# A three-layer kernel on one core: first token block undivided, six pairs of w_in prepared in it, and a maximum in the weight conversion

## Chip, cores and metric

The kernel runs on one core of a Trainium2 chip. The metric is the device time of one execution in microseconds; the time before is the median of three runs.

## What is computed

The reference runs a linear attention over 8 batches of 8 heads (576 tokens, head dimension 64), and then two dense layers over the 4608 tokens, with a SiLU and with a hard swish. Inputs are fp32; the weights reach the chip as 64-bit numbers.

```python
q_s = np.exp(q - q.max(-1, keepdims=True)); q_s = q_s / (q_s.sum(-1, keepdims=True) + 1e-09)
k_s = np.exp(k - k.max(2, keepdims=True));  k_s = k_s / (k_s.sum(2, keepdims=True) + 1e-09)
kv = np.einsum('bhsd,bhse->bhde', k_s, v)
x = np.einsum('bhsd,bhde->bhse', q_s, kv)          # then laid out as 4608 x 512
h = x @ w_in;  x = (h / (1 + np.exp(-h))) @ w_out            # 512 -> 2048 -> 512
h = x @ w2_in; out = (h * np.clip(h + 3, 0, 6) / 6) @ w2_out
```

## The kernel before

Tokens go in nine blocks of 512: eight hold the first 512 tokens of a batch, the ninth the remaining 64 of each. A layer has 8 pairs p of hidden slices (2 x 128). A *cycle* g is one pair of one block of one layer: 144 cycles, of which the first 8 (`first_cycle`) are block 0 of layer 1 and the other 136 (`cycle`) all the rest. A cycle computes the first product of its pair (x times w_in) into the PSUM banks A, B and C, the activation of both halves (`bend`), and, one cycle late, the second product (`layer_out`, called G(0) to G(7)) of the pair before, into four accumulating banks y.

Exactness is kept by splitting an fp32 operand into a rounded high part and the remainder (`split`: a cast on ScalarE, then a subtraction on VectorE), and doing three matmuls for one (`mm3`, lines 73 to 75). In `cycle` the first product is done as seven half-size products in place of eight (`product` 1 to 7), which needs sums of x (`sums_x`), their splits (`operand_x`), and sums of w_in (`operands_w`: four additions or subtractions of 256 columns, a split of 768 columns and one of 1024), kept in one of two `ring` tiles. `prepare_in(p)` makes such a ring tile and `keep_w` writes it to DRAM (`wd`); later blocks read it back with `load_w(g)`, two cycles ahead.

Block 0 is different. Its second product is one full fp32 matmul (line 550, which the trace shows as two instructions), on weights that are not split. Its first product (`plain_in`) is undivided in the sense of the seven products, but each factor is split: x by `at_xhalf` into op tiles, w_in by `plain_w` into a ring tile. Pairs 0 and 1 are made ready for the later blocks in cycles 6 and 7, pairs 2 to 7 in the cycles 8 to 13 of block 1, two cycles before their use; block 1 uses all eight from the ring tile where they were made, without reading them back.

Weights arrive as 64-bit bit patterns (`feed`, 1 MB each), and `converting` makes fp32 of them: an absolute value of the high word on ScalarE (line 103), then on VectorE a shift (104), the sign (109), the low word's bits (114), and a multiplication by a comparison, which sets tiny weights to zero (121). These steps lie between `yield`s; `pump(k)` advances the oldest unfinished generator by k steps at fixed places in a cycle.

Attention for later blocks runs in between. Unit u is one pair of heads of one batch (32 units). `plan` gives each of its steps a tick relative to x_at(u), eight ticks a cycle, and `run(tick)` issues them at the place `side(k)`. A maximum `nm` is sent to DRAM and read back as a row for all partitions (`at_shift`, tile nb), which GpSimd adds (`at_sub`) before an exponential (`at_exp`). For units from batch `TURNED` on, q also arrives turned, and its maximum `qm` and reciprocal sum `qr` go through DRAM too (`send`, `at_spread`); for the units before, q is transposed on TensorE (`at_trq`). Loads, sends and reads are issued by SyncE's queue, in program order, each waiting there for what it needs; for units not turned, nm is sent from ScalarE's queue.

The order inside a cycle is written out by hand: each engine runs its instructions in program order.

## Time and profile before

| | us |
|---|---|
| median of three runs (1780.19 to 1785.1) | 1783.17 |
| profiled execution | 1791.71 |
| its span, first to last instruction | 1789.9 |
| TensorE busy | 1671.2 |
| VectorE busy | 1070.6 |
| ScalarE busy | 733.9 |

The profiled execution is 1.8 us longer than its span. A stage's limit is found by looking at that stage alone, since the shares of the whole span mix stages that have different limits. The times of single rows below are from that one execution.

### The profile page before, as it was taken

Reading aid. Unit: us, or ns where it says so; the run is one execution under the profiler, and the core shown is the slowest. Engines: PE = TensorE matmul, PEld = TensorE weight load, DVE = VectorE, ACT = ScalarE, POOL = GpSimd, SP = SyncE. Lnnn points to the kernel's source line nnn. Section 1 sums busy time; section 2 is a strip of 40 time slices with the busy share of each in tenths; the row PEclk is TensorE's granted clock in tenths of the full one; section 3 lists DMA queues with packets and bytes.
Section 4 is the critical chain, followed back from the end, with each engine's and each line's share of the span. In section 5 each row is a group of like instructions: output and inputs, shape, how many; then the busy total and the mean of one; then the engine's idle time right before and its main releaser. Section 6 shows DMA issues by size and latency. Waiting matters only on the chain.

```text
span 1789.9 us, 25567 instructions
## 1 busy us (share of the span) xinstructions
PE 1671.2 (93%) x10076; PEld 1442.6 (81%) x10076; DVE 1070.6 (60%) x1753; ACT 733.9 (41%) x1400; POOL 181.2 (10%) x124
## 2 busy tenths in 40 slices
PE   6797999998999999999999899999999999999994
PEld 5565777787888888788877788888888888888884
DVE  6899887474665757458878764444354535353531
ACT  5343555344354444344444433333333333343421
POOL 3231112222222222210000000000000000000000
PEclk9899999999999999999999999999999999999997
DMA  6453549999999999858886845464545464555540
GB/s 209 150 198 126 198 165 282 208 235 244 249 228 248 257 251 237 224 204 322 329 340 249 328 172 212 165 222 185 222 165 212 179 233 179 204 192 203 210 166 24
DMA packets 68383, 386.03 MB, mean 216 GB/s; under 512 B 18856, under 2 KB 22440, under 8 KB 43432
## 3 DMA queue, kind: packets, MB, share of 16 engines
q1 hardware_dynamic: 65960, 369.72, 64.6%
q10 hardware_dynamic: 2304, 14.69, 2.0%
q8 instruction: 80, 1.31, 0.3%
q14 instruction: 39, 0.32, 0.1%
HBM read 335.94 MB, written 48.43 MB: 215 GB/s over the span
## 4 chain that ended last, share of the span: by engine, by line
PE 67%; DVE 18%; DMA 6%; ACT 5%; issue 2%; SPq 0%; POOL 0%; ACTq 0%; DVEq 0%; POOLq 0%
PE y L73 11%; PE y L74 11%; PE y L75 10%; PE B L73 6%; PE B L75 5%; PE B L74 5%; PE A L73 4%; PE A L75 4%; PE A L74 4%; DMA qr<-qr 3%; DVE gs L70 2%; DMA ring<-wd 2%; DVE g L529 1%; PE C L74 1%; PE C L75 1%
## 5 line engine op out<-in xcount | busy, mean ns | idle before, releaser
L70 DVE TENSOR_TENSOR gs<-g,gs 128x512 fp32r<-128x512 f32 x272 | 207.6, 763 | 158.4 <-ACT gs L69 155.9
L73 PE MATMUL B<-o,ring 128*128 128x256 f32 x816 | 249.6, 306 | 53.3 <-DVE s L673 31.1
L73 PE MATMUL A<-op,ring 128*128 128x256 f32 x880 | 254.3, 289 | 6.3 <-ACT ring L161 3.2
L69 ACT CAST gs<-g 128x512 fp32r<-128x512 f32 x272 | 168.6, 620 | 206.1 <-DVE g L529 199.0
L74 PE MATMUL A<-op,ring 128*128 128x256 f32 x880 | 250.8, 285 | 1.9 <-DVE op L70 1.9
L73 PEld LDWEIGHTS B<-o,ring 128*128 128x128 f32 x816 | 155.6, 191 | 120.0 <-DVE B L683 42.8
L75 PE MATMUL A<-op,ring 128*128 128x256 f32 x880 | 250.9, 285 | 0.8 <-DVE ring L162 0.8
L75 PE MATMUL B<-o,ring 128*128 128x256 f32 x816 | 232.2, 285 | 0.0
L74 PE MATMUL B<-o,ring 128*128 128x256 f32 x816 | 232.1, 284 | 0.0
L74 PE MATMUL y<-wol,gs 128*128 128x512 f32 x576 | 227.5, 395 | 0.0
L73 PE MATMUL y<-woh,gs 128*128 128x512 f32 x576 | 227.3, 395 | 0.0
L75 PE MATMUL y<-woh,gs 128*128 128x512 f32 x576 | 224.4, 390 | 0.0
L73 PE MATMUL y<-gs,woh 128*128 128x512 f32 x512 | 205.9, 402 | 0.0
L673 DVE TENSOR_TENSOR s<-B,s 128x256 f32<-128x256 f32 x136 | 57.4, 422 | 245.0 <-PE B L75 244.3
L74 PE MATMUL y<-gs,woh 128*128 128x512 f32 x512 | 203.6, 398 | 0.0
L75 PE MATMUL y<-gs,wol 128*128 128x512 f32 x512 | 201.5, 394 | 0.0
L73 PEld LDWEIGHTS A<-op,ring 128*128 128x128 f32 x880 | 170.2, 193 | 16.5 <-ACT ring L161 3.7
L74 PEld LDWEIGHTS A<-op,ring 128*128 128x128 f32 x880 | 170.2, 193 | 9.0 <-DVE op L70 2.1
L75 PEld LDWEIGHTS A<-op,ring 128*128 128x128 f32 x880 | 170.2, 193 | 1.0 <-DVE ring L162 1.0
L74 PEld LDWEIGHTS B<-o,ring 128*128 128x128 f32 x816 | 156.3, 192 | 9.7 <-issue 0.5
L75 PEld LDWEIGHTS B<-o,ring 128*128 128x128 f32 x816 | 156.4, 192 | 0.0
L527 ACT ACTIVATE g<-A,half 128x512 f32<-128x512 f32 x72 | 49.5, 687 | 253.7 <-DVE A L678 253.7
(151 smaller groups left out, 3036.8 us busy)
## 6 DMA issues: line engine op xcount, KB each, us to landing
ring<-wd SPq DMA_DIRECT2D x128, 1792.0 KB, 7.4
st<-w_dram SPq DMA_DIRECT2D x32, 1024.0 KB, 7.4
ev<-kv_dram SPq DMA_DIRECT2D x28, 640.0 KB, 9.3
wd<-ring SPq DMA_DIRECT2D x8, 1792.0 KB, 5.9
wd<-r ACTq DMA_DIRECT2D x8, 1792.0 KB, 9.5
kq<-kqT_dram SPq DMA_DIRECT2D x20, 576.0 KB, 8.4
q<-qn_dram SPq DMA_DIRECT2D x32, 288.0 KB, 8.8
yd<-y SPq DMA_DIRECT2D x9, 1024.0 KB, 11.7
```

The lines of the kernel that those rows point to most:

```text
L69: nc.scalar.copy(hi, src)
L70: nc.vector.tensor_tensor(out=lo, in0=src, in1=f32(hi), op=ALU.subtract)
L73: nc.tensor.matmul(o, lhsT=wh, rhs=xh, start=start, stop=False, **kw)
L74: nc.tensor.matmul(o, lhsT=wh, rhs=xl, start=False, stop=False, **kw)
L75: nc.tensor.matmul(o, lhsT=wl, rhs=xh, start=False, stop=stop, **kw)
L527: nc.scalar.activation(out=a, in_=hb, func=AF.Relu, scale=1.0 / 6.0, bias=half)
L529: nc.vector.scalar_tensor_tensor(out=a, in0=a, scalar=1.0, in1=hb, op0=ALU.add if m == 0 else ALU.min, op1=ALU.mult)
L673: nc.vector.tensor_tensor(out=s2, in0=B_[:, lo], in1=s5, op=ALU.add)
```

## The change

- Block 0's first product becomes eight full fp32 matmuls of 512 columns a cycle, on the converted weights (`raw_in`) and on x as it is copied from PSUM (`first_x`). `plain_w` and the splits of block 0's x go.
- `prepare_in` for pairs 0 to 5 runs in cycles 1 to 6, and the result goes to DRAM; block 1 reads these six back with `load_w`. Pairs 6 and 7 are made ready in cycles 12 and 13.
- In `converting` the comparison and multiplication at the end go; instead VectorE raises the absolute value to SMALLEST (`tensor_scalar_max`) before the shift. A weight below it becomes that small number instead of zero.
- `TURNED` becomes 2: the q of batch 2 arrives turned as well.
- Plans: units of block 1 start later and are spaced differently; `nm` is sent two ticks after its maximum, and for units not turned ScalarE's queue also issues the read back. For turned units sends are steps of their own, and most steps are one or two ticks earlier.
- In `cycle`, G(4) stands ahead of product 4, and `load_w` directly behind it.

The diff, without the hunks that only follow from these:

```diff
@@ -23,7 +23,7 @@
 KC = DM // P
 QP, QJ = 96, 6
 EPS = 1e-9
-TURNED = 3
+TURNED = 2
 U32 = mybir.dt.uint32
 SMALLEST = 1.125 * 2.0 ** -15
 HT = TB // 2
@@ -94,15 +94,13 @@
     def converting(w, m, p, i):
         t = staged.pop((m, p, i))
         low, high = t[:, :, 0], t[:, :, 1]
-        q = z_p if m == 0 else m2_p[0]
-        if m == 0:
-            bits = q.tile([P, 2 * DM], U32, tag="z2", name="bits")
-        else:
-            bits = w.bitcast(U32)
-        ok = q.tile([P, 2 * DM], F32, tag="z3" if m == 0 else "ok", name="ok")
-        nc.scalar.activation(out=ok, in_=f32(high), func=AF.Abs)
+        bits = w.bitcast(U32)
+        size = (z_p if m == 0 else m2_p[0]).tile([P, 2 * DM], F32, tag="z3" if m == 0 else "ok", name="size")
+        nc.scalar.activation(out=size, in_=f32(high), func=AF.Abs)
+        yield
+        nc.vector.tensor_scalar_max(size, size, SMALLEST)
         nc.vector.tensor_scalar(
-            out=bits, in0=high, scalar1=3, scalar2=0x3FFFFFF8,
+            out=bits, in0=size.bitcast(U32), scalar1=3, scalar2=0x3FFFFFF8,
             op0=ALU.logical_shift_left, op1=ALU.bitwise_and,
         )
         yield
@@ -115,12 +113,8 @@
             out=bits, in0=low, scalar=29, in1=bits,
             op0=ALU.logical_shift_right, op1=ALU.bitwise_or,
         )
-        yield
         if m == 0:
             feed()
-        nc.vector.scalar_tensor_tensor(
-            out=w, in0=ok, scalar=SMALLEST, in1=f32(bits), op0=ALU.is_ge, op1=ALU.mult
-        )
 
     active = []
 
@@ -141,11 +135,6 @@
     def convert_in(p):
         raw_in[p] = w = w_pool[p].tile([P, 2 * DM], F32, tag=f"a{p}", name="wi")
         yield from converting(w, 0, p, 0)
-        if p:
-            yield
-            low = plain_w(p)
-            yield
-            low()
 
     def convert_out(p):
         raw_out[p] = w = w_pool[p].tile([P, 2 * DM], F32, tag=f"b{p}", name="wo")
...
@@ -178,13 +161,14 @@
 
     def keep_w(m, p, r):
         wd[m, p] = d = dram.tile([P, 14 * 256], F32, tag=f"wd{m}{p}", name="wd")
-        e = nc.scalar if m else nc.sync
-        e.dma_start(out=d, in_=f32(r).rearrange("p h s n -> p (h s n)"))
+        nc.sync.dma_start(out=d, in_=f32(r).rearrange("p h s n -> p (h s n)"))
 
     def prepare_in(p):
         r = ring_tile(NC + p)
         s = z_p.tile([P, 2 * DM], F32, tag="z2", name="s")
         yield from operands_w(r, raw_in.pop(p), s)
+        yield
+        yield
         keep_w(0, p, r)
 
     def split_out(m, p, w):
...
@@ -296,14 +282,10 @@
         k, q = s["k"], s["q"]
         nm = sm_p.tile([P, 1], F32, tag="nm", name="nm")
         nc.vector.tensor_reduce(out=nm, in_=k, axis=AX.X, op=ALU.max, negate=True)
-        if not ahead(u):
-            s["nd"] = nd = dram.tile([1, P], F32, tag="nm", name="nmd", bufs=4)
-            (nc.sync if turned(u) else nc.scalar).dma_start(out=nd.rearrange("o p -> p o"), in_=nm)
         ks = sm_p.tile([P, 1], F32, tag="ks", name="ks")
         qm = sm_p.tile([QP, QJ * 2, 1], F32, tag="qm", name="qm")
         nc.vector.tensor_reduce(out=qm, in_=q, axis=AX.X, op=ALU.max, negate=True)
-        if turned(u):
-            send(s, "qm", qm)
+        s["qm"] = qm
         nc.gpsimd.tensor_tensor(
             out=q, in0=q, in1=qm.to_broadcast([QP, QJ * 2, D]), op=ALU.add
         )
@@ -316,10 +298,16 @@
     def at_qexp(u):
         nc.scalar.activation(out=un[u]["q"], in_=un[u]["q"], func=AF.Exp)
 
+    def at_sendnm(u):
+        s = un[u]
+        s["nd"] = nd = dram.tile([1, P], F32, tag="nm", name="nmd", bufs=4)
+        (nc.sync if turned(u) else nc.scalar).dma_start(out=nd.rearrange("o p -> p o"), in_=s["nm"])
+
     def at_shift(u):
         s = un[u]
         s["nb"] = nb = ld_p.tile([P, 1, P], F32, tag="nb", name="nb", bufs=1)
-        nc.sync.dma_start(out=nb.rearrange("p o d -> p (o d)"), in_=s["nd"].to_broadcast([P, P]))
+        e = nc.sync if turned(u) else nc.scalar
+        e.dma_start(out=nb.rearrange("p o d -> p (o d)"), in_=s["nd"].to_broadcast([P, P]))
 
     def at_sub(u):
         s = un[u]
...
@@ -432,8 +420,7 @@
             (kh, kl), (qh, ql) = s["kv"], s["qT"]
             mm3(bx[:, :n], kh, kl, qh[:, sl], ql[:, sl], True, True)
         if b == 0:
-            o = op_x[(1, 2)[c // 2] if i == 0 else (5, 3)[c // 2]]
-            split(o[:, 0, c % 2], o[:, 1, c % 2], bx[:, :HT])
+            nc.scalar.copy(first_x(c)[:, i * HT:(i + 1) * HT], bx[:, :HT])
         else:
             nc.scalar.copy(x_raw(b)[:, c, i * HT:(i + 1) * HT], bx[:, :HT])
         if i:
...
@@ -503,16 +499,10 @@
                 start and k == 0, k == 1, skip_group_check=True,
             )
 
-    def plain_in(g, j, o, h):
-        r = ring[g]
+    def plain_in(g, j, o):
         for k in range(KC):
-            w = (1, 2)[k // 2] if j == 0 else (3, 0)[k // 2]
-            x = op_x[((1, 2), (5, 3))[h][k // 2]]
-            sl = slice((k % 2) * P, (k % 2 + 1) * P)
-            mm3(
-                o[:, h * HT:(h + 1) * HT], r[:, 0, w, sl], r[:, 1, w, sl], x[:, 0, k % 2], x[:, 1, k % 2],
-                h == 0 and k == 0, k == KC - 1, skip_group_check=True,
-            )
+            w = (((1, 2), (3, 0))[j][k // 2] * 2 + k % 2) * P
+            nc.tensor.matmul(o, lhsT=raw_in[g][:, w:w + P], rhs=first_x(k), start=k == 0, stop=k == KC - 1)
 
     def bend(g, j, hb):
 
@@ -590,21 +580,22 @@
 
     def x_at(u):
         b, c = divmod(u, NP)
-        return 16 + 12 * c if b == 1 else 64 * (b - 1) + 16 * c + 4
+        return 19 + 11 * c if b == 1 else 64 * (b - 1) + 16 * c + 4
 
     for u in range(NP, NU):
         x = x_at(u)
-        at(x_at(u - 2) - 3 if u - 2 >= NP else -90, at_load, u)
+        at(x_at(u - 2) - 5 if u - 2 >= NP else -90, at_load, u)
         if turned(u):
             plan = [
-                (-27, at_soft), (-26, at_kexp), (-24, at_qexp), (-23, at_knorm), (-22, at_norm),
-                (-19, at_shift), (-19, at_spread, "qm"), (-13, at_spread, "qr"),
-                (-12, at_sub), (-12, at_tadd), (-9, at_exp), (-9, at_texp), (-7, at_tmul), (-4, at_tsplit),
+                (-28, at_soft), (-27, at_kexp), (-26, at_sendnm), (-26, at_send, "qm"), (-25, at_qexp),
+                (-24, at_knorm), (-23, at_norm), (-21, at_shift), (-21, at_spread, "qm"),
+                (-20, at_send, "qr"), (-15, at_spread, "qr"), (-14, at_tadd), (-13, at_sub),
+                (-10, at_texp), (-9, at_exp), (-8, at_tmul), (-4, at_tsplit),
             ]
         else:
             plan = [
-                (-24, at_soft), (-22, at_kexp), (-21, at_shift), (-20, at_qexp), (-19, at_knorm),
-                (-18, at_norm), (-17, at_sub), (-13, at_exp), (-11, at_trq, 0), (-9, at_trq, 1),
+                (-19, at_soft), (-18, at_sendnm), (-17, at_kexp), (-16, at_qexp), (-15, at_shift), (-14, at_knorm),
+                (-13, at_norm), (-12, at_sub), (-9, at_exp), (-9, at_trq, 0), (-8, at_trq, 1),
             ]
         plan += [(-6, at_kv), (-4, at_kvsplit), (0, at_xhalf, 0), (2, at_xhalf, 1)]
         for d, fn, *args in plan:
@@ -627,15 +618,15 @@
         last = p == NC - 1 and g + 1 < N
         G = lambda k: layer_out(g - 1, k)
         late = LATE <= g < PER + NC
-        early = n == 1 and p < NC - 2
+        early = n == 1 and NC - 4 <= p < NC - 2
         if early:
             active.append(prepare_in(p + 2))
 
         def side(k):
 
             run(8 * g + k)
-            if early and k >= 5:
-                pump(1)
+            if n == 1 and k >= 4:
+                pump(2 if k == 5 else 1)
             if late and g > LATE:
                 pump({NC - 2: (1, 0, 0, 0, 1, 1, 0, 0), NC - 1: (1, 0, 0, 0, 0, 1, 0, 0)}.get(p, (2, 0, 0, 0, 1, 1, 2, 0))[k])
             if p == NC - 2 and g + 2 < N and k in (6, 7):
@@ -684,18 +675,18 @@
         next(ba)
         G(3)
         side(3)
+        G(4)
         product(g, 4, B_[:, lo], False)
+        if g + 2 < N and not early:
+            load_w(g + 2)
         for _ in ba:
             pass
         next(bc)
         next(bc)
-        G(4)
         side(4)
-        if g + 2 < N and g + 2 >= 2 * NC:
-            load_w(g + 2)
+        G(5)
         for _ in bc:
             pass
-        G(5)
         side(5)
         G(6)
         side(6)
...
@@ -720,34 +711,36 @@
 
         if g + 1 < NC:
             active.append(convert_in(g + 1))
+        else:
+            load_w(NC)
         active.append(convert_out(g))
-        if g >= NC - 2:
-            active.append(prepare_in(g + 2 - NC))
+        if 0 < g < NC - 1:
+            active.append(prepare_in(g - 1))
         ba, bc = bend(g, 0, A), bend(g, 1, B_)
-        plain_in(g, 0, A, 0)
+        plain_in(g, 0, A)
         side(0)
-        plain_in(g, 0, A, 1)
         next(ba)
         side(1)
-        G(0)
-        G(1)
+        plain_in(g, 1, B_)
         for _ in ba:
             pass
         side(2)
-        plain_in(g, 1, B_, 0)
+        G(0)
+        next(bc)
         side(3)
-        plain_in(g, 1, B_, 1)
-        next(bc)
-        side(4)
+        G(1)
         G(2)
-        G(3)
         for _ in bc:
             pass
+        side(4)
+        G(3)
+        G(4)
         side(5)
-        G(4)
+        if g == NC - 1:
+            load_w(NC + 1)
         G(5)
+        G(6)
         side(6)
-        G(6)
         G(7)
         side(7)
 
...
```

## Rows read from the trace of the kernel before

**Rows 1.** The page: busy us (share of the span) and instructions of two engines

```profile
PE 1671.2 (93%) x10076; PEld 1442.6 (81%) x10076; DVE 1070.6 (60%) x1753; ACT 733.9 (41%) x1400; POOL 181.2 (10%) x124
```

**Rows 2.** Stretches: length, busy us (instructions) of each engine, then columns of the header

```profile
core 0: us, PE busy (x) PEld busy (x) DVE busy (x) ACT busy (x) POOL busy (x), PEclk, DMA share, GB/s
34.20:175.50 141.30, 116.25 (x594) 83.52 (x595) 124.00 (x145) 56.31 (x91) 32.65 (x16) 0.93 0.43 149
175.50:290.70 115.20, 103.63 (x610) 85.76 (x611) 94.80 (x156) 61.38 (x118) 21.17 (x13) 0.97 0.59 196
292.10:800.20 508.10, 483.06 (x2945) 422.61 (x2944) 302.48 (x538) 226.08 (x479) 116.76 (x75) 0.98 0.92 236
800.20:1049.70 249.50, 230.66 (x1387) 197.86 (x1386) 200.57 (x297) 112.72 (x187) 0.00 (x0) 0.99 0.79 302
1049.70:1751.40 701.70, 701.70 (x4357) 623.67 (x4357) 319.92 (x567) 250.48 (x470) 0.00 (x0) 1.00 0.53 195
```

**Rows 3.** Timeline, first product: start us, us, what [idle before <-releaser]

```profile
35.49 0.47 PE L75 MATMUL A<-op,ring 128*128 128x256 f32 x1 [0.76 <-DVE ring L162]
```

**Rows 4.** Timeline, cycle 0 to 1

```profile
51.30 0.74 ACT L331 ACTIVATE ev<-ev 128x640 f32<-128x640 f32 x1 [10.42 <-POOL ev L327]
...
53.81 0.74 PE L369 MATMUL D<-ident,q 96*128 96x96 f32 x3 [10.53 <-ACT qf L384]
```

**Rows 5.** VectorE's groups, 34.2 to 175.5: busy us, mean ns | idle before

```profile
L121 DVE SCALAR_TENSOR_TENSOR wi<-ok,bits 128x1024 f32<-128x1024 f32 x7 | 13.7, 1950 | 0.2
...
L162 DVE TENSOR_TENSOR ring<-wi,ring 128x1024 fp32r<-128x1024 f32 x8 | 10.1, 1259 | 10.4 <-ACT ring L161 10.4
```

**Rows 6.** Timeline of an undisturbed cycle of layer 2

```profile
1523.61 0.38 PE L73 MATMUL B<-o,ring 128*128 128x256 f32 x1
1523.83 0.28 PE L74 MATMUL B<-o,ring 128*128 128x256 f32 x1
1523.95 0.28 PE L75 MATMUL B<-o,ring 128*128 128x256 f32 x1
...
1528.08 0.36 ACT L662 COPY B<-A 128x256 f32<-128x256 f32 x1 [1.32 <-PE A L75]
```

**Rows 7.** The chain that ended last, cycle 1: start us, us, what

```profile
59.70 1.72 PE y L550 x4
```

**Rows 8.** VectorE's groups, 800.2 to 1049.7

```profile
L121 DVE SCALAR_TENSOR_TENSOR w<-ok,w 128x1024 f32<-128x1024 f32 x16 | 19.5, 1221 | 0.4
...
L104 DVE TENSOR_SCALAR w<-st 128x1024 uint32<-128x1024 uint32 x16 | 11.0, 690 | 0.2
```

**Rows 9.** VectorE's groups, 175.5 to 290.7

```profile
L70 DVE TENSOR_TENSOR ring<-s,ring 128x1024 fp32r<-128x1024 f32 x7 | 8.6, 1222 | 0.5 <-ACT ring L69 0.5
L172 DVE TENSOR_TENSOR s<-wi 128x256 f32<-128x256 f32 x12 | 7.6, 631 | 0.0
...
L70 DVE TENSOR_TENSOR ring<-wi,ring 128x768 fp32r<-128x768 f32 x6 | 5.7, 944 | 0.0
...
L172 DVE TENSOR_TENSOR s<-wi,s 128x256 f32<-128x256 f32 x6 | 2.5, 418 | 0.0
```

**Rows 10.** DMA issues, whole span: KB each, median us to landing

```profile
nmd<-nm ACTq DMA_DIRECT2D x8, 0.5 KB, 8.1
```

**Rows 11.** Stretches: three pieces of the attention blocks

```profile
316.10:333.60 17.50, 13.15 (x74) 11.61 (x73) 6.28 (x12) 4.89 (x12) 4.37 (x3) 0.90 0.92 196
333.60:357.20 23.60, 23.60 (x150) 20.93 (x149) 12.65 (x24) 10.33 (x23) 4.49 (x4) 1.00 0.86 213
419.50:438.40 18.90, 14.40 (x75) 12.70 (x74) 6.58 (x12) 4.83 (x12) 4.32 (x3) 0.82 0.88 230
```

**Rows 12.** Timeline, cycles 16 to 18

```profile
304.24 1.09 SPq L272 DMA_DIRECT2D qr<-qr  x2
...
321.88 1.40 POOL L284 TENSOR_TENSOR kq<-kq,qr 128x576 f32<-128x576 f32 x1 [11.57 <-DMA qr<-qr]
...
325.36 0.39 PE L73 MATMUL B<-o,ring 128*128 128x256 f32 x1 [4.35 <-DVE s L673]
```

**Rows 13.** DMA issues, 292.1 to 800.2

```profile
ring<-wd SPq DMA_DIRECT2D x40, 1792.0 KB, 13.6
```

**Rows 14.** SyncE's waits: who <- for what: us in total, times, longest

```profile
SPq L322 <- DMA nmd<-nm: 106.9, 18, 14.0
```

More of the change, by code (lines that the diff above doesn't have):

```diff
@@ L156, in ring_tile @@
         return ring[g]
-    def plain_w(p):
-        r = ring_tile(p)
-        src = raw_in[p].rearrange("p (s n) -> p s n", s=4)
-        nc.scalar.copy(r[:, 0, :4], src)
-        return lambda: nc.vector.tensor_tensor(out=r[:, 1, :4], in0=src, in1=f32(r[:, 0, :4]), op=ALU.subtract)
     def operands_w(r, w, s):
@@ L259, in at_load_v, with at_send @@
         nc.sync.dma_start(out=s["v"].rearrange("p j d -> p (j d)"), in_=kv5[b, c, :, 5 * P:])
-    def send(s, key, t):
+    def at_send(u, key):
+        s = un[u]
+        t = s[key]
         s[key] = d = dram.tile([2, QP, QJ], F32, tag=key, name=key, bufs=4)
@@ L317, in at_qexp @@
         nc.scalar.activation(out=un[u]["q"], in_=un[u]["q"], func=AF.Exp)
+    def at_sendnm(u):
+        s = un[u]
+        s["nd"] = nd = dram.tile([1, P], F32, tag="nm", name="nmd", bufs=4)
+        (nc.sync if turned(u) else nc.scalar).dma_start(out=nd.rearrange("o p -> p o"), in_=s["nm"])
     def at_shift(u):
@@ L348, in at_norm @@
         if turned(u):
-            send(s, "qr", qr)
+            s["qr"] = qr
             return
@@ L440, in at_xhalf @@
             nc.scalar.copy(rest[:, c, b * 64:(b + 1) * 64], bx[:, HT:n])
-    op_x = {i: x_p.tile([P, 2, 2, HT], F32R, tag=f"op{i}", name=f"op{i}") for i in (1, 2, 3, 5)}
+    op_x = {}
+    x0 = {}
     xr = {}
@@ L453, in x_raw, with first_x @@
         return xr[n]
+    def first_x(c):
+        k = c // 2
+        if k not in x0:
+            x0[k] = x_p.tile([P, 2, TB], F32, tag=f"op{k + 1}", name="x0")
+        return x0[k][:, c % 2]
     def load_y(n):
@@ L472, in operand_x @@
             op_x[4] = z_p.tile([P, 2, 2, HT], F32R, tag="z1", name="o4")
+        if i not in op_x:
+            op_x[i] = x_p.tile([P, 2, 2, HT], F32R, tag=f"op{i}", name=f"op{i}")
         x, t = x_raw(n), tx[n]
@@ L709, in side @@
             run(8 * g + k)
-            pump(2 if k in (2, 5) else 1)
+            pump(2 if k in (1, 2, 4, 6) else 1)
             if g == NC - 1:
@@ L713, in side @@
                     sums_x(1, k - 2)
-                for i in {3: (7,), 4: (6, 1, 2), 5: (4, 5), 6: (3,)}.get(k, ()):
+                for i in {3: (5,), 4: (1, 6), 5: (2, 3), 6: (7, 4)}.get(k, ()):
                     operand_x(1, i)
@@ L813, in attention_two_mlps @@
             at_x(2)
-            pump(2)
+            pump(1)
             at_x(3)
-            plain_w(0)()
         w_b = pool("w_b", 1)
```

## Prediction

> **What bounds the kernel now.** I read the whole-run view first, to see which engine is busiest: TensorE 93%, VectorE 60% [rows 1]. That is a mean over stages, so the stages come next, from the table of stretches [rows 2], where each engine's busy time is set against the length. In the first block (34.2 to 175.5) VectorE works 124.0 of 141.3 us, in the second (175.5 to 290.7) 94.8 of 115.2. In the next five blocks TensorE has 483 of 508 and the DMA engines stand at a share of 0.92. Where w2 is converted (800 to 1050) TensorE has 231 of 250 and VectorE 201. After 1050 TensorE is never idle. So the change has to be priced stage by stage: VectorE and its helpers in the first two blocks, single waits later, TensorE's own work at the end.
>
> Two waits stand out in the first block. The first product's third matmul waits until 35.49 us for the last half of a split weight [rows 3]. And TensorE stands still for 10.5 us, until 53.8: it waits for a copy on ScalarE, queued behind an exponential for which ScalarE had waited 10.4 us, for GpSimd and behind that for a DMA [rows 4].
>
> **Start.** The split of pair 0 goes (its VectorE half alone is 1.26 us [rows 5]), and so do eight subtractions for x between the conversion's steps. What is late next is the conversion's last step and the last copy of x. Without that split and the subtractions the first product should start near 31 us instead of 35.5: **-4.5 us** (0 to -6).
>
> **First block, TensorE.** A cycle's first product is 48 matmuls of 256 columns now. In a run they start 0.12 us apart [rows 6], 5.8 us in all. The whole one is 8 products of 512 columns in full fp32. The second product of this block shows that price: 1.72 us for four instructions, two to a product [rows 7], so 0.86 us each and 6.9 us a cycle. That is +1.1 us on each of 8 cycles, +9 us. The products alone then take 103 us (8 x 6.9 and 56 second ones at 0.86); today's busy time of 116.3 plus 9 would be 125, but that holds stretches at 1.2 GHz (granted clock 0.93 in the mean [rows 2]). I take 114 between them, below VectorE's sum in the next part, so the 9 us lie beside VectorE's work; if that cover goes they count in full.
>
> **First block, VectorE.** Removed: eight splits of w_in, 10.1 us; the last step of a conversion, 1.95 us in the mean for w_in, where GpSimd works beside it [rows 5], and 1.22 us where it doesn't [rows 8]. Added per conversion: a maximum with one input. No fp32 maximum is in the trace. Its nearest rows are the one-input shift on 1024 elements, 0.69 us, and the two-input step, 1.22 us [rows 8]. I take 0.69, because the maximum has one input and one constant as the shift has; the gain is 0.53 on each of 15 conversions, 8 us, and zero by the other end. The Trainium skill, "VectorE: DVE Perf Modes", in its perf-mode tier table, gives one-input fp32 operations in SBUF twice the rate of two-input ones; by that rate the 8 us would stand.
>
> Moved in: making pairs 0 to 5 ready, of which one and a half fell in this block before. One costs four additions or subtractions of 0.42 (up to 0.63 in the mean beside GpSimd), a split of 0.95 and one of 1.22 [rows 9], 3.9 us; four and a half more are +17.5 us. The sum is -10.1 - 8 + 17.5 - 0.9 (a transposed q no longer split) = -1.5, about 122 us of VectorE work.
>
> VectorE's idle time, 17.3 us of the 141.3, should shrink. About 7 lay in the stall of [rows 4]: unit 4's exponential sat in tick 3 and moves to tick 10, while its maximum now starts in tick 0, so some nine ticks (16 us) lie between the send of the maximum and the exponential. Another 5.8 us or so were waits for ScalarE's copies of split weights, which are gone. New waits: ScalarE now issues the read back of the maximum, and must wait in its queue until the send has landed, 8.1 us [rows 10], while the plan leaves three ticks, about 6 us. Queued behind it on ScalarE are the absolute values of the next conversion and the tanh, for which VectorE waits, and TensorE behind VectorE. I count 1 to 2 us for each of four units, and 3 us in all for the copies between the new subtractions: 122 busy and about 12 idle are 134 instead of 141.3, **-7 us** (-27 if TensorE alone set it, +25 if ScalarE's waits were not covered).
>
> Six writes to DRAM and two reads of 1.8 MB join the queue of SyncE. Each write is issued two steps late, so the feeds behind it need not wait for the split; the DMA share was 0.43 in this block [rows 2], so I cost them at nothing. If that cover goes, a feed lands after its conversion is due and each write costs its own landing.
>
> **Second block.** The making ready that leaves takes 4.5 x 4 = 18 us from VectorE's 94.8, leaving about 77. Six w_in loads take the place of operands made in place; they are issued nearly two cycles ahead. What is late next is TensorE: two undisturbed attention cycles last 23.6 us [rows 11], so eight are 94.4. With some 8 us of waits at the block's ends: 102 instead of 115.2, **-13 us** (-20 to -5). Batch 2's q now comes turned: 24 transposes less on TensorE, two sends and four broadcast reads more a unit, as the later blocks have them.
>
> **Blocks three to seven.** The cycle from 316.1 to 333.6 lasts 17.5 us against 11.8 for half a pair [rows 11]. Read backwards: TensorE waited 4.35 us for VectorE, which was behind a split of q that needed GpSimd, and GpSimd had waited 11.6 us for the broadcast read of qr, issued at 304.24 us just behind the write of y [rows 12]. Two like it begin at 419.5 and 723.6 us; three times 5.7 are some 17 us. The new plan issues that read two ticks earlier, ahead of the write of y. From issue to the split are 11 ticks instead of 9, about 16 us; without the write in front I take the stall as gone. The next part's order gives 4 us more here. Against both stand the DMA share of 0.92 [rows 2] and weight loads that need 13.6 us in the median [rows 13]: the same bytes in less time leave 0.95 or more. I take **-15 us** (0 to -25) of the 21, the rest lost to later landings.
>
> **G(4) ahead of product 4.** In an undisturbed cycle product 4 starts its second matmul 0.22 us after the first, where the next follow at 0.12 [rows 6]: it waits for the sum into B. One more G (three starts, 0.70 us) hides that: 0.09 us in each of the 66 cycles after 1050, **-6 us**. The price: the second half's tanh comes some 0.6 us later, and so does the cast that stands on ScalarE ahead of the copy into B. That copy had 1.32 us of idle time before it [rows 6], so it has room. Where w2 is converted the room is often gone: 16 maxima save 8.5 us of VectorE work there, and the later tanh costs up to 0.5 us in some 20 cycles: **0** (-8 to +8).
>
> **Sum.** -4.5 - 7 - 13 - 15 - 6 = -45.5. The profiled execution took 1791.7 us (1789.9 of span, 1.8 around it), so it would take 1746; it is 8.5 us above the median of 1783.2, and I carry that over: **1738 us**.
>
> **The rivals.** (a) The DMA engines hold the attention blocks: what GpSimd no longer waits for, the products wait for, at weight loads. For it: share 0.92, loads of 13.6 us; against: TensorE is busy 483 of 508 us, so loads come in time as yet. The 15 us go: 1753. (b) ScalarE stands for the full landing of 8.1 us at each of four read backs, +32: 1770. For it: SyncE waited 107 us for such landings in 18 cases, 14.0 at most [rows 14]; against: about 6 us of work lie between. The Trainium skill, "DMA: Bandwidth & Descriptors", in its anatomy of one DMA, says that a DMA's semaphore wait is served on the sequencer that issues it, before dispatch; by that rule the 1770 could come, and the waits on SyncE's queue agree with it. (c) The first block runs at TensorE's 114 us: 20 less, 1718. (d) Slower: the move of product 4 makes the second half's tanh the bound of every cycle. That costs 0.61 us (0.70 less 0.09) in 136 cycles, 83: 1821. It decides from the point where ScalarE's copy has under 0.7 us to spare; the 1.32 us speak against it. (e) Nothing measurable: maxima cost 1.22 us, making ready goes on beside GpSimd at 5 us, and the first block gives back what the others gain: 1783.
>
> **How the numbers follow.** Forecast 0.48, (a) 0.20, (b) 0.13, (c) 0.10, (d) 0.05, (e) 0.04. The range takes in the forecast, (a), (b) and (c): 1710 to 1770. Within 0.3% (5.3 us, about what a measurement can tell from no change) lies (e), slower (d), faster the rest: 0.91, 0.04, 0.05.
>
> **What would show it.** A first product near 31 us with no gap of 10 us after it; a first block of about 134 us with VectorE over 85% busy; maxima of 0.69 us; a second block near 102 us; no cycle of 17 us between 300 and 800; 10.54 us a cycle at the end. It would be wrong if ScalarE idles 5 us or more before the read back of the maximum, if products wait for ring loads, or if ScalarE's copy into B follows directly on its cast.

## The result, and the profile after

The changed kernel takes 1764.6 us (median of four runs, 1764.4 to 1769.1) where the kernel before took 1784.1 in the same session: a ratio of 0.9899, interval 0.9876 to 0.9923. It is faster by 19.5 us. The forecast was 1738, some 45 us faster; the sign was right, the size less than half of what was forecast. In a later group of runs the same two kernels lie only 6.6 us apart (1789.4 against 1796.0, ratio 0.9964; the run stands below), so the size is that of one session.

The page's line on the two busiest engines, after (as [rows 1]), and then the view of stretches, cut where the stages change (as [rows 2]; lengths, busy us and instructions of each engine, granted clock, DMA share, GB/s):

```profile
PE 1659.3 (94%) x9796; PEld 1423.1 (81%) x9796; DVE 1044.0 (59%) x1733; ACT 739.9 (42%) x1392; POOL 185.4 (11%) x128
```

```profile
31.30:176.60 145.30, 124.83 (x338) 60.25 (x339) 122.10 (x162) 58.39 (x95) 29.70 (x17) 0.92 0.85 239
176.60:281.50 104.90, 97.97 (x589) 83.33 (x588) 79.08 (x130) 56.92 (x110) 28.38 (x16) 0.99 0.83 229
281.50:772.60 491.10, 477.07 (x2956) 422.64 (x2955) 296.27 (x535) 228.72 (x478) 116.03 (x76) 0.99 0.94 244
772.60:1028.60 256.00, 230.35 (x1388) 200.88 (x1387) 194.61 (x297) 114.76 (x188) 0.00 (x0) 0.99 0.78 295
1028.60:1723.80 695.20, 695.20 (x4352) 628.04 (x4351) 325.76 (x567) 256.63 (x469) 0.00 (x0) 1.00 0.53 197
```

To compare stages between kernels I cut every trace at the same five events: the first product, and ScalarE's copy into B at the head of cycles 8, 16, 56, 77 and 143. The first two columns below are the two profiled executions; "forecast" is the term of the prediction.

| stage | before | after | change | forecast |
|---|---|---|---|---|
| start | 34.2 | 31.3 | -2.9 | -4.5 |
| first block | 142.5 | 145.3 | +2.8 | -7 |
| second block | 115.4 | 104.9 | -10.5 | -13 |
| blocks three to seven | 508.0 | 491.2 | -16.8 | -15 |
| w2 converted (cycles 56 to 76) | 249.6 | 255.9 | +6.3 | 0 |
| cycles 77 to 142 | 701.6 | 695.3 | -6.3 | -6 |
| rest | 38.5 | 38.6 | 0 | 0 |
| span | 1789.9 | 1762.4 | -27.5 | -45.5 |

So of the 18 us by which the spans miss the forecast, 9.8 lie in the first block and 6.3 where w2 is converted. A further 8 us lie between the spans (-27.5) and the medians (-19.5).

**The first block after.** The view of waits (31.3 to 176.6; who, on what, us in total, times, longest) shows a wait that the kernel before didn't have, at the top:

```profile
ACT size L99 <- DMA st<-w_dram: 23.8, 7, 8.7
DVE size L101 <- ACT size L99: 14.9, 5, 5.9
POOL ev L315 <- DMA nb<-nmd: 10.5, 2, 6.5
PE D L357 <- ACT qf L372: 8.6, 2, 8.1
ACT size L99 <- DMA nmd<-nm: 7.1, 2, 5.8
ACT ring L69 <- DMA nmd<-nm: 4.1, 1, 4.1
```

ScalarE, about to take the absolute value, stands 23.8 us before feeds of raw weights have landed, and VectorE stands behind it. (Where a wait has two reasons, the view names the one that came last.) The DMA issues of that stretch (KB each, median us to landing), first after, then before:

```profile
st<-w_dram SPq DMA_DIRECT2D x13, 1024.0 KB, 11.0
wd<-ring SPq DMA_DIRECT2D x6, 1792.0 KB, 13.0
nmd<-nm ACTq DMA_DIRECT2D x4, 0.5 KB, 10.0
```

```profile
st<-w_dram SPq DMA_DIRECT2D x13, 1024.0 KB, 4.9
wd<-ring SPq DMA_DIRECT2D x1, 1792.0 KB, 5.6
```

A feed of the same 1 MB lands after 11.0 us instead of 4.9. The timeline of one cycle shows how that can count (start us, us, what, idle before and its releaser):

```profile
117.57 1.24 DVE L112 SCALAR_TENSOR_TENSOR wo<-st,wo 128x1024 uint32<-128x1024 uint32 x1
118.87 0.33 SPq L90 DMA_DIRECT2D st<-w_dram  x1
...
129.77 1.15 ACT L99 ACTIVATE size<-st 128x1024 f32<-128x1024 f32 x1 [3.53 <-DMA st<-w_dram]
...
132.61 5.29 SPq L90 DMA_DIRECT2D st<-w_dram  x2
...
135.87 1.23 DVE L112 SCALAR_TENSOR_TENSOR wo<-st,wo 128x1024 uint32<-128x1024 uint32 x1
...
148.75 1.16 ACT L99 ACTIVATE size<-st 128x1024 f32<-128x1024 f32 x1 [1.99 <-DMA st<-w_dram]
```

There are two staging tiles. A feed is issued when the conversion that read its tile has ended (117.57 + 1.24 = 118.81, issued at 118.87), its conversion starts 10.9 us later, when it lands (129.77), and ends at 137.10; the next feed into that tile (the second of the two from 132.61 to 137.90) follows at once, and its conversion starts at 148.75. From start to start that is 19.0 us for two conversions, which are the work of one cycle: a ring of a landing and a conversion. It is little longer than TensorE's own work, though, which fills 16.9 us of these 19.0 (view of stretches):

```profile
129.77:148.75 18.98, 16.89 (x51) 8.49 (x52) 14.56 (x23) 7.50 (x12) 0.00 (x0) 1.00 0.97 222
```

The stall of [rows 4] is back as well, 8 us instead of 10.5 (same view, cycles 0 and 1):

```profile
38.93 0.83 ACT L299 ACTIVATE q<-q 96x768 f32<-96x768 f32 x1
43.85 0.33 ACTq L310 DMA_DIRECT2D nb<-nmd  x1
...
48.49 1.12 ACT L99 ACTIVATE size<-st 128x1024 f32<-128x1024 f32 x1 [8.72 <-DMA st<-w_dram]
...
53.75 0.74 ACT L319 ACTIVATE ev<-ev 128x640 f32<-128x640 f32 x1 [3.65 <-POOL ev L315]
54.39 0.38 ACT L372 COPY qf<-D 128x288 f32<-128x288 f32 x1
...
54.82 0.74 PE L357 MATMUL D<-ident,q 96*128 96x96 f32 x3 [8.08 <-ACT qf L372]
```

ScalarE ends a step at 39.8, is held until 43.85 by the read back that it issues (which waits for the send of the maximum), then until 48.49 by a feed, then until 53.75 by GpSimd, and only then copies the q for which TensorE waits. The chain that ended last (start us, us, what) goes through the maximum, not through the feed: its send, its read back and GpSimd's addition together take 18.5 us.

```profile
35.09 8.75 DMA nmd<-nm
43.85 7.83 DMA nb<-nmd
51.83 1.90 POOL ev L315
```

**Later stages.** In cycles 56 to 76 TensorE's waits at bank B, after and then before (view of waits):

```profile
PE B L73 <- DVE s L664: 13.2, 10, 2.3
PE B L73 <- ACT B L653: 12.3, 8, 2.4
```

```profile
PE B L73 <- ACT B L662: 9.5, 8, 1.7
PE B L73 <- DVE s L673: 9.3, 10, 2.1
```

Together 25.5 us instead of 18.8: 6.7 more, against 6.3 for the stage. At the end the change does what was said: product 4's second matmul starts 0.12 us after its first, not 0.22 as in [rows 6], and ScalarE's copy still has 0.65 us to spare:

```profile
1498.66 0.28 PE L73 MATMUL B<-o,ring 128*128 128x256 f32 x1
1498.78 0.28 PE L74 MATMUL B<-o,ring 128*128 128x256 f32 x1
...
1502.36 0.36 ACT L653 COPY B<-A 128x256 f32<-128x256 f32 x1 [0.65 <-PE A L75]
```

### The profile page after: what moved, and what is told of

Read it like the earlier page. It is cut to its first block, busy times and chain, and to the rows that moved or that the text cites. A ratio compares the mean times of both kernels' runs of the same rounds, so it can differ in the third digit from the quotient of the medians.

```text
span 1762.4 us, 25043 instructions
## 1 busy us (share of the span) xinstructions
PE 1659.3 (94%) x9796; PEld 1423.1 (81%) x9796; DVE 1044.0 (59%) x1733; ACT 739.9 (42%) x1392; POOL 185.4 (11%) x128
## 4 chain that ended last, share of the span: by engine, by line
PE 67%; DMA 14%; DVE 11%; ACT 4%; issue 2%; SPq 1%; POOL 0%; ACTq 0%; DVEq 0%; POOLq 0%
PE y L73 11%; PE y L74 11%; PE y L75 11%; PE B L73 5%; PE B L75 5%; PE B L74 5%; PE A L73 4%; DMA ring<-wd 4%; PE A L74 4%; PE A L75 4%; DMA q<-qn_dram 3%; DMA nmd<-nm 2%; DMA st<-w_dram 2%; PE C L75 1%; PE C L73 1%
## 5 line engine op out<-in xcount | busy, mean ns | idle before, releaser
L70 DVE TENSOR_TENSOR gs<-g,gs 128x512 fp32r<-128x512 f32 x272 | 195.3, 718 | 151.7 <-ACT gs L69 150.6
L73 PE MATMUL B<-o,ring 128*128 128x256 f32 x816 | 234.7, 288 | 37.3 <-DVE s L664 24.2
L73 PE MATMUL A<-op,ring 128*128 128x256 f32 x816 | 232.7, 285 | 12.6 <-DMA ring<-wd 10.4
L74 PE MATMUL A<-op,ring 128*128 128x256 f32 x816 | 232.1, 284 | 1.2 <-DVE op L70 1.1
L75 PE MATMUL A<-op,ring 128*128 128x256 f32 x816 | 231.7, 284 | 0.0
L75 PE MATMUL B<-o,ring 128*128 128x256 f32 x816 | 230.7, 283 | 0.0
L74 PE MATMUL B<-o,ring 128*128 128x256 f32 x816 | 230.4, 282 | 0.0
L73 PEld LDWEIGHTS A<-op,ring 128*128 128x128 f32 x816 | 156.7, 192 | 22.7 <-ACT o L69 4.2
L74 PEld LDWEIGHTS A<-op,ring 128*128 128x128 f32 x816 | 156.9, 192 | 7.5 <-DVE op L70 2.1
L75 PEld LDWEIGHTS A<-op,ring 128*128 128x128 f32 x816 | 157.0, 192 | 0.0
## 6 DMA issues: line engine op xcount, KB each, us to landing
wd<-r SPq DMA_DIRECT2D x8, 1792.0 KB, 10.5
```

Source lines behind the costliest of these rows:

```text
L70: nc.vector.tensor_tensor(out=lo, in0=src, in1=f32(hi), op=ALU.subtract)
L73: nc.tensor.matmul(o, lhsT=wh, rhs=xh, start=start, stop=False, **kw)
L74: nc.tensor.matmul(o, lhsT=wh, rhs=xl, start=False, stop=False, **kw)
L75: nc.tensor.matmul(o, lhsT=wl, rhs=xh, start=False, stop=stop, **kw)
```

## The experiments

They ran in three groups of four, where the kernel before takes 1802.0, 1810.0 and 1796.0 us (medians; the first and third on one chip, the second on another). Ratios are to the kernel before in the same group, and stage lengths come from each run's profile. As a yardstick: four traces that share the changed kernel's code up to cycle 8 have first blocks of 143.7 to 147.8 us.

**The order of G(4), alone.** On the kernel before:

```diff
+        G(4)
         product(g, 4, B_[:, lo], False)
+        if g + 2 < N and g + 2 >= 2 * NC:
+            load_w(g + 2)
...
-        G(4)
         side(4)
-        if g + 2 < N and g + 2 >= 2 * NC:
-            load_w(g + 2)
+        G(5)
         for _ in bc:
             pass
-        G(5)
```

So "the order" is three moves in one, here and in the runs that put it back: G(4), the load of weights, and G(5), which now stands before the last steps of the second half's activation. They were not tried one by one.

> The kernel before with one part of the change alone: G(4) ahead of product 4, as in the changed kernel. Theory A (the forecast's term holds where TensorE sets the pace, and the later tanh costs where w2 is converted): 6 us less after the conversion of w2, 2 to 4 less in the attention blocks, 5 to 8 us more where w2 is converted: 1780 to 1784 against some 1784. Rival (the order costs nothing there, the loss in that stage comes from the other steps of the conversion): that stage stays at 249 to 251 us, the whole at 1774 to 1776.

Measured: 1811.4, ratio 1.0049 (1.0030 to 1.0068), slower. Cycles 77 to 142 take 695.3 us, -6.3 as forecast. But cycles 56 to 76 take 262.8 us, where the two traces of the kernel before have 249.6 and 252.9: some 10 to 13 us lost, more than the end gains.

**The changed kernel with the old order**, in all cycles, and then in cycles 56 to 79 alone:

> The changed kernel with the order of G(4) and product 4 as before. Theory A (the order cost the w2 stage): that stage falls from 256 to 247 to 250 us, the stage after it rises by 6 and the attention blocks by 2 to 5: the whole 1763 to 1769. Rival (another part cost the stage): it stays at 255 to 257 and the whole rises to 1773 to 1777.

Measured: 1787.8, ratio 0.9907 (0.9879 to 0.9936); cycles 56 to 76 take 245.9 us, where the changed kernel has 255.9 and a run beside this one with the changed order (the read back on SyncE's queue, below) 255.8; 77 to 142 take 701.6 again.

```diff
+        if not late:
+            G(4)
         product(g, 4, B_[:, lo], False)
...
+        if late:
+            G(4)
         side(4)
...
```

> The changed kernel with the order of G(4) and product 4 as before in the cycles from 56 to 79, where w2 is converted, and the new order elsewhere. Theory A: that stage falls from 256 to 246 us, the stage after it keeps its 695: 10 us less than the changed kernel, 1.5% under the kernel before. Rival (the cost of the order wanders to the edges of the stage): 2 us or less.

Measured: 1794.2, ratio 0.9923 (0.9896 to 0.9950); 244.5 us in cycles 56 to 76 and 696.2 in 77 to 142. The two kernels beside it with the changed order take 255.9 and 257.9 us in the former. So all three kernels say the same: one order pays at the end, the other where w2 is converted.

**The maximum, alone.** `converting` as in the changed kernel, all else as before.

> The kernel before with one part alone: the maximum in place of the comparison at the end of a conversion. Theory A: 0.5 us less VectorE work in each of 15 conversions shows in the first block, 4 to 8 us less there, and nothing (within 2 us) where w2 is converted: 1776 to 1780. Rival (the second step, now 1.4 us in place of 1.2, lies in the chain of the w2 stage): that stage grows from 250 to 254 us or more, the whole 1780 to 1784.

Measured: 1793.4, ratio 0.9952 (0.9929 to 0.9975): 8.6 us less. First block 139.6 (142.5 and 144.4 in the two traces of the kernel before, 145.0 in the kernel with the order alone, whose code is the same up to cycle 8). The maximum in VectorE's groups of this kernel's first block, and one of its conversions beside GpSimd and one without (the timeline):

```profile
L101 DVE TENSOR_SCALAR size<-size 128x1024 f32<-128x1024 f32 x15 | 13.6, 904 | 3.3 <-ACT size L99 3.2
```

```profile
84.66 0.69 DVE L101 TENSOR_SCALAR size<-size 128x1024 f32<-128x1024 f32 x1 [0.18 <-ACT size L99]
91.27 1.82 DVE L101 TENSOR_SCALAR size<-size 128x1024 f32<-128x1024 f32 x1
```

Eleven of the fifteen take 0.63 to 0.69 us, as taken from [rows 8] (ten of them with GpSimd idle); the other four, 1.36 to 1.82, all run while GpSimd does, so the mean is 0.90. The rule of the Trainium skill that the prediction weighed ("VectorE: DVE Perf Modes", perf-mode tier table: one-input fp32 steps at twice the rate of two-input ones) agrees where GpSimd is idle.

**Without the move of the six pairs.** The changed kernel with pairs 2 to 7 made ready in block 1 again, from the ring, as before:

```diff
-        early = n == 1 and NC - 4 <= p < NC - 2
+        early = n == 1 and p < NC - 2
...
-        if g + 2 < N and not early:
+        if g + 2 < N and g + 2 >= 2 * NC:
...
-        if 0 < g < NC - 1:
-            active.append(prepare_in(g - 1))
+        if g >= NC - 2:
+            active.append(prepare_in(g + 2 - NC))
...
```

> The changed kernel without the move: pairs 0 and 1 made ready in cycles 6 and 7, the others in block 1 as before, no reading back there. Theory C (writes and their queue make the feeds late): the first block falls from 145 to 125 to 132 us, the feeds land after about 5 us as before, and block 1 rises from 105 to about 115. Rival D (full fp32 products make TensorE the bound of the first block): the block stays within 5 us of 145 and TensorE is busy over 90% of it.

Measured: 1809.1, ratio 1.0001 (0.9983 to 1.0020). The second block takes 122.2 us, where the kernel with the order by stage, which has the move and ran beside it, takes 111.7. The first takes 143.2 against its 147.8: 12 us of VectorE's work less (106.2 busy instead of 118.3) and four writes less give only 4.6. So VectorE's sum, from which the forecast was made, is not what bounds the first block. Theory C missed as well: the feeds do land sooner, after 6.4 us, but the block doesn't fall to 125 to 132, and ScalarE's waits for them are no shorter than the 23.8 us above (first block; DMA issues and waits):

```profile
st<-w_dram SPq DMA_DIRECT2D x13, 1024.0 KB, 6.4
```

```profile
ACT size L99 <- DMA st<-w_dram: 26.0, 6, 9.6
```

Rival D comes closest: the block stays, with TensorE busy 87% of it (it said over 90%). The kernel before ran in the same group, on the same chip. The stretch of the first block in it, and then in this kernel:

```profile
34.72:179.08 144.36, 117.57 (x599) 84.40 (x599) 127.14 (x147) 57.32 (x93) 32.01 (x16) 0.93 0.45 146
```

```profile
31.00:174.22 143.22, 124.70 (x338) 60.00 (x339) 106.21 (x138) 51.52 (x87) 27.49 (x17) 0.93 0.62 165
```

Feeds land alike (7.3 us before, 6.4 here), and pairs 0 and 1 are made ready in this block in both. VectorE has 21 us less to do, TensorE 7 us more, and the block is 1.1 us shorter.

**The read back on SyncE's queue.**

```diff
-        e = nc.sync if turned(u) else nc.scalar
-        e.dma_start(out=nb.rearrange("p o d -> p (o d)"), in_=s["nd"].to_broadcast([P, P]))
+        nc.sync.dma_start(out=nb.rearrange("p o d -> p (o d)"), in_=s["nd"].to_broadcast([P, P]))
```

> The changed kernel with the read back of nm issued by SyncE for all units, as before, instead of ScalarE. Theory B (ScalarE standing for the landing is what the first block lost): the block falls from 145 to 136 to 140 us: 1756 to 1760. Rival C (the feeds of weights are late, as they share the queue with six more writes): SyncE waits for the landing in ScalarE's place, feeds behind it land later, and the block stays at 145 or grows to 150: 1764 to 1770.

Measured: 1786.3, ratio 0.9922 (0.9888 to 0.9955); first block 147.7 us, no shorter than with the wait on ScalarE. ScalarE no longer waits for nmd; it waits for feeds instead, which queue behind the read back now (waits of this kernel's first block, ScalarE's and then SyncE's queue's own):

```profile
ACT size L99 <- DMA st<-w_dram: 32.5, 8, 8.6
```

```profile
SPq L309 <- DMA nmd<-nm: 15.8, 4, 5.8
```

So the edit doesn't remove the wait, it moves it, and neither shows nor excludes what the wait costs. Rival (b)'s mechanism is there, as the Trainium skill has it ("DMA: Bandwidth & Descriptors", anatomy of one DMA: the sequencer that issues a DMA waits for its semaphore): the wait moves with the queue, 15.3 us on ScalarE in the changed kernel (11.2 in three cases, and the 4.1 from 39.8 to 43.85 above), 15.8 in four on SyncE here. That is not the 32 that full landings would give.

**Five of the six writes left out.** Only pair 0's operands are written; block 1 and later blocks read those for pairs 1 to 5 as well, so the first layer's products of these pairs are other numbers.

```diff
     def keep_w(m, p, r):
+        if m == 0 and 0 < p < 6:
+            wd[m, p] = wd[0, 0]
+            return
```

> The changed kernel with only pair 0 written to DRAM of the six; the reads of pairs 1 to 5 read pair 0's, so these pairs' products are not the reference's. All work on VectorE stays. Theory C: the five writes of 1.8 MB are the cause; without them feeds land after 5 to 8 us, ScalarE's wait for them falls from 24 to under 8, and the first block from 145 to 133 to 138. Rival (VectorE's added work is the cause): the block stays at 143 to 146.

Measured: 1796.6, ratio 0.9935 (0.9910 to 0.9961); first block 142.9 against 147.8 beside it, and ScalarE's waits for feeds fall to 9.8 us, nearly all in the one of 9.4 at 48 us; one of 8.2 us behind a load of k is new. Feeds land after 9.3 us, not the 5 to 8 of theory C, and the block misses its 133 to 138. So the writes costed at nothing cost some 5 us at most: 4.9 here, from one execution each, where kernels alike up to there differ by 4.1.

**What sets the first block: two edits apart.** The first takes unit 4's exponential out of ScalarE's way (from tick 10 to tick 12, behind both copies of the turned q); the second takes the feeds away from the fourth on. They ran with the changed kernel beside them.

```diff
-(-12, at_sub), (-9, at_exp), (-9, at_trq, 0),
+(-12, at_sub), (-7 if u == NP else -9, at_exp), (-9, at_trq, 0),
```

> The changed kernel with unit 4's exponential two ticks later, so that ScalarE copies the turned q before it waits for the maximum read back. TensorE's gap of 8 us at 54.8 us should fall to 4 or less in any case. Theory T (TensorE's own 124.8 us and its four gaps set the first block): the block gets shorter by 4 to 6 us, to about 140. Theory S (two staging tiles: a feed is issued when the conversion two before it has ended, lands 11 us later, and a cycle of two conversions so lasts 17 to 18 us): the feed that lands at 48.4 us still sets the second cycle, and the block stays within 2 us of the changed kernel's beside it.

```diff
         for m, p, i in stream[:k]:
+            if m == 0 and fed[0] > 2:
+                fed[0] += 1
+                staged[m, p, i] = last_fed[fed[0] % 2]
+                continue
...
```

> The changed kernel in which only the first three feeds of the first layer's weights are loaded; the other thirteen conversions read the two tiles that are already there, so the dense weights are wrong and 13 MB of loads are gone, everything else is as in the changed kernel. Theory S: ScalarE's waits for feeds (23.8 us) go, the cycle is no longer bound by the feed's landing, and the first block falls to 130 to 135 us, TensorE's 124.8 busy and what is left of its gaps. Theory T (TensorE and the read backs of the maxima set it): it falls by 4 us or less, to 141 or more. Rival (b) of the prediction: the waits for the maximum's read back, 7 to 8 us each, remain on ScalarE and then are the only long ones.

> The changed kernel once more, as the yardstick for the three beside it: about 0.99 of the kernel before; start near 31 us, first block 143 to 148 us, stage in which w2 is converted 255 to 257 us, 695 us from cycle 77 to 142.

Measured: the changed kernel 1789.4, ratio 0.9964 (0.9948 to 0.9980), first block 145.9; the later exponential 1788.1, ratio 0.9959 (0.9941 to 0.9978), first block 144.3, TensorE's gap 4.4 us instead of 9.1; the feeds gone 1774.4, ratio 0.9886 (0.9861 to 0.9911), first block 136.3. Without the feeds the block is 9.6 us shorter, and its engines are busy as before. Stretch and ScalarE's waits for the maximum in that kernel's first block:

```profile
31.90:168.20 136.30, 124.75 (x338) 59.89 (x339) 123.25 (x161) 58.32 (x95) 29.68 (x16) 0.95 0.58 149
```

```profile
ACT size L105 <- DMA nmd<-nm: 8.6, 3, 4.6
```

Half of a stall was taken out and 1.6 us came of it, which tells nothing beside a spread of 4; 13 loads were taken out and 9.6 came of it. So the feeds cost some 10 us of the block, as theory S says and theory T doesn't. They cost it at the block's two ends: TensorE's idle time falls from 21.9 to 11.6 us, of which 5.2 in the gap near 55 us (9.1 to 4.0) and 4.4 where the last operands of the next block are late (4.8 to 0.4). Between the two ends its waits are about the same, 7.3 and 6.6 us. And the edit doesn't separate the ring from the traffic: without 13 MB of loads the maximum's read back, too, lands after 3.5 us instead of 7.8. What is left, 136.3, lies just above the 130 to 135 expected: TensorE is busy 124.8 us of it and VectorE 123.3, and ScalarE's three waits for nmd make 8.6.

**A faster kernel.** Two of these edits together in the changed kernel: the order by stage and the later exponential, whose diffs stand above.

> The changed kernel with two edits: unit 4's exponential two ticks later, behind the two turns of its q, and the old place of G(4) in the 24 cycles around the conversion of w2. If the two costs found so far are separate and real, it is faster than the changed kernel beside it by 10 us for the order (255.9 to 245 us in that stage) and by 0 to 6 us for the exponential, so a ratio near 0.985 of the kernel before where the changed one has 0.99. If the order's 10 us are given back elsewhere, it stands level with the changed kernel.

Measured: 1773.4, ratio 0.9878 (0.9859 to 0.9897), where the changed kernel has 0.9964 beside it: 16 us faster than that. By stages: cycles 56 to 76 take 245.7 us instead of 257.5, the first block 141.4 instead of 145.9, cycles 77 to 142 take 696.2 instead of 695.3. TensorE's waits at bank B in cycles 56 to 76 fall from 13.2 and 12.4 us to

```profile
PE B L73 <- DVE s L664: 8.0, 9, 2.0
PE B L73 <- ACT B L653: 7.8, 6, 1.7
```

that is by 9.8 of the 11.8 us.

**The kernel before once more.**

> The kernel before, unchanged, for its stages on this chip. If the difference between the profiled execution that the forecast started from and the median lies in the attention blocks (waits for DMA), the blocks three to seven differ from 508 us and the stage after 1050 stays at 702; if it lies elsewhere, the first block or the w2 stage differs from 142 or 250.

Measured: 1813.0. Blocks three to seven take 524.8 us on this chip, where the profiled execution that the forecast started from has 508.0; every other stage agrees within 3.5 us.

## Why the prediction was wrong

**Start: right.** The first product starts at 31.3 us (sign: near 31). The gain is 2.9, not 4.5, because I measured from the third matmul at 35.49 [rows 3], while the stage began with the first, at 34.2.

**First block: two steps failed, "I take 114 between them, below VectorE's sum" and "I cost them at nothing".** VectorE's sum was right: 122.1 us against about 122. But the block's length doesn't follow it: in the run without the move VectorE had 21 us less to do than in the kernel before, and the block was 1.1 us shorter. TensorE, priced between 103 and 125 us, takes 124.8, the upper end, and is the busiest engine of the block. So its 9 us more did not lie beside VectorE's work, the cover of which the prediction said "if that cover goes they count in full", and rival (c), 114, was never open. As a sum, the 134 forecast are 114 and 20 us in which TensorE waits; measured are 124.8 and 20.5. No run takes the full fp32 products out, so their share of the miss is argued from these busy times, not shown.

The other step: six writes and two reads were costed at nothing because the DMA share was 0.43 [rows 2]. It became 0.85, a feed's landing rose from 4.9 to 11.0 us, and "if that cover goes, a feed lands after its conversion is due" came true. Five writes less bring 4.9 us, about half of the 9.8 by which the block misses, but hardly more than the 4.1 by which like kernels differ. With all feeds gone the block is 136.3 us, near the forecast of 134, but the feeds were there before the change too, so this says what late feeds can cost and not what the writes did.

The stall of [rows 4] was said to vanish because nine ticks, 16 us, lie between the send and the exponential. TensorE had gone through these ticks in 11.6 us (from the send at 35.1 to 46.7, where its gap begins), and send, read back and addition took 18.5, of which the prediction had priced only the send. With the exponential two ticks later 4.4 of 9.1 us are left, behind the feed. ScalarE's waits for the sends were counted as 4 to 8 us; they make 15.3, still far from the 32 of rival (b).

**Second block: right.** -10.5 against -13, within its -20 to -5. The run without the move shows that the move is what makes it (122.2 against 111.7); it costs 4.6 in the first block. Beside other traces of before the gain is smaller: 114.2 against 111.0 and 111.7 on one chip, which is outside the range, 115.0 (the maximum alone) against 106.4 to 109.4 on the other.

**Blocks three to seven: mechanism right, size partly luck.** The cycles of 17.5 and 18.9 us of [rows 11], and the third of 18.5, are gone; the longest but one is now 14.2. The read of qr lands after 5.5 us in the median instead of 12.3, and TensorE's waits at bank B for VectorE's s fall; before, and then after:

```profile
PE B L73 <- DVE s L673: 20.2, 9, 4.5
```

```profile
PE B L73 <- DVE s L664: 5.2, 5, 1.3
```

One cycle grew from 14.9 us to 16.8 (564.2 to 581.0; 16.3 to 19.6 in six of the nine other runs of the changed kernel and its variants), and in it a first product waits 3.2 us for ring weights, the sign that the prediction gave for being wrong here. In the profiled execution the stage gives 16.8 us. But part is given back as rival (a) said: products wait for weight loads. TensorE's wait for them in this stage, after, then in the changed kernel of the third group, and in the kernel with the maximum alone, which ran on the same chip as that:

```profile
PE A L73 <- DMA ring<-wd: 7.0, 6, 3.2
```

```profile
PE A L73 <- DMA ring<-wd: 18.4, 9, 3.6
```

```profile
PE A L73 <- DMA ring<-wd: 0.5, 2, 0.3
```

On that chip the stage takes 512.2 us against 518.8, a gain of 6.6 with 18 us of new waits; but the kernel before with the order alone takes 511.9 there, so either the order makes that gain, or single executions of this stage differ by as much. On the other chip (order by stage against the kernel before) it takes 521.9 against 524.8, with 29.9 us of such waits where there were 3.0. VectorE meets the same: it waits 37.6 us for kq from DRAM, where it waited 0.3 before:

```profile
DVE nm L284 <- DMA kq<-kqT_dram: 37.6, 14, 6.3
```

So the forecast's likeliest case and rival (a) are both there, in shares that differ from run to run; that the stage came out within 2 us of its -15 is partly luck.

**Conversion of w2: the term "0 (-8 to +8)" was mis-sized.** It is +6.3, and the order costs 10 to 13. The prediction let 8.5 us of saved VectorE work stand against "up to 0.5 us in some 20 cycles", which is 10, and called it even. The second is shown by kernels that differ in the order (9.9 and 11.8 within a group, 11.4 and 13.4 in the other, 10 to 13 on the kernel before). Of the first less is there: the maximum alone leaves this stage at 248.2 us, 1.4 and 4.7 less than the two traces of before, and the changed kernel with the old order in this stage at 244.5, 8.4 less than the kernel before beside it (245.9 and 245.7 in the other runs). So 1.4 to 8.4 us stand against 10 to 13. Rival (d) named the mechanism and put it in every cycle; it acts where w2 is converted and not in the last cycles, where 0.65 us are left of the room of 1.32 us [rows 6].

**Last cycles: right.** -6.3 against -6, 10.53 us a cycle against 10.54.

**The 8.5 us carried over.** I took the offset of the profiled execution over the median as a constant. The profiled execution of before lay 7.6 us above its median of 1784.1; that of after (1764.5) lies on its own. So 27.2 us between the profiled executions are 19.5 between medians. The sum was made against a long execution of before, and the cycles that the change mends may partly be what made it long: blocks three to seven are the stage that varies most between runs of one code (508.0 and 524.8 in the kernel before, 491.2 and 512.2 in the changed one). Where the 7.6 us lay can't be seen from one trace, and stays open.

Not tried: the second layer's writes, which moved from ScalarE's queue to SyncE's and which the prediction didn't price. With the old order the stage that holds them is 4 us shorter than before (245.9 against 249.6), so a large cost in them is unlikely.

## What to carry to other kernels

Before a stage is priced by one engine's sum, work out the others' at the upper end of their range as well: here TensorE's 125 us lay above the 122 of VectorE on which the term was built. Before a transfer is costed at nothing, look for the ring that it stands in: here, with two staging tiles, a load was issued only when a tile was free, and its landing was part of a cycle's time, which a mean DMA share of 0.43 had not told. An order that saves a wait where TensorE is the only bound can cost more where ScalarE or VectorE come last, so test it by stage, and keep each order where it pays. And a gain in a stage that lives on DMA landings is to be read on more than one execution and more than one chip.

## What the runs showed of the hardware

The landing of a load of 1 MB rose from 4.9 to 11.0 us as the share of busy DMA engines rose from 0.43 to 0.85, and a write of 1.8 MB from 5.6 to 13.0. In between a load took 6.4 us at 0.62 (no move) and 9.3 at 0.72 (one write), but also 7.3 at 0.45 (the kernel before, run once more). The Trainium skill ("DMA: Bandwidth & Descriptors", anatomy of one DMA, a fit for the GpSimd path) gives a fixed 2.0 us and the bytes at 436 GB/s, by which 1 MB would be an estimated 4.4: near the 4.9 of the block with little traffic, far from the 11.0 of the full one. One-input steps of VectorE lose much beside GpSimd: the maximum takes 0.69 us alone and up to 2.01 beside it in the changed kernel. And identical code differs by chip and by session: the kernel before took 1784.1, 1796.0, 1802.0 and 1810.0 us (medians), while cycles 77 to 142, in which TensorE never waits, took 701.6 us in both of its traces.
